# Sparse attention into a gated FFN: PSUM banks taken singly or in pairs, and a new order for the first 420 tasks

## The chip, the cores and the metric

The kernel runs on one core of a Trainium2 chip. A core has five engines that run side by side, each through its own queue of instructions in order: PE (TensorE, matrix products), ACT (ScalarE, functions of one input), DVE (VectorE, elementwise work and reductions), POOL (GpSimd, here only the issue of loads) and SP (SyncE, here the issue of stores and of transposes by DMA). They hand work on through semaphores. PE writes into PSUM, eight banks of 128 partitions by 512 float32 values; ACT and DVE read it from there. A *whole-array* matmul contracts over 128 rows; a *row tile* uses 64 rows, and two of them run side by side. The trace shows these as `128*128` and `64*128`.

The metric is the device time of one execution in microseconds (us), the median of several.

## The reference

Block-sparse attention over `q`, `k`, `v` of shape 4 x 8 x 768 x 64 (batch, heads, tokens, width), then a gated FFN on the 3072 x 512 tokens that come out of it:

```python
mask = np.abs(blk_i - blk_j) <= window          # blocks of 32 tokens
mask = mask | (blk_i == 0) | (blk_j == 0) | (blk_i == n_blocks - 1) | (blk_j == n_blocks - 1)
for qb in range(n_blocks):
    for kb in sampled_blocks[qb]:
        mask[qb * block:(qb + 1) * block, kb * block:(kb + 1) * block] = True
attn = softmax(where(mask, q @ k.T / 8, -1e9))
x = (attn @ v) as tokens x 512
gate = 1 / (1 + exp(-(x @ w_gate)))
out = (gate * (x @ w_val)) @ w_out              # 512 -> 1536 -> 512
```

## The kernel before

**Units.** The work is cut into twelve units: batch `b` of 4 times query third `u` of 3 (256 queries). In a unit the eight heads go by pairs `p` of 4. A pair has three steps `j` of 256 keys each. A step is: a score job on PE (`Step.qk`, L556 on), the exponential on ACT (L586, 128 x 1024 from two banks to float16), and a multiplication with the mask on DVE (L592). For the first unit the mask is a bias that PE adds ahead of the scores, so that a score job there has eight matmuls and no multiplication. When the three steps of a pair are done, PE forms the product with `v` (`Pair.pv` for the first two units, whole-array; `Pair.pv_parts` later, row tiles), DVE divides by the sums (`norm`, L655 and L656; before it `fold`, L646, for the later units), and the result is turned, by PE and a copy for the first two units (`turn`, `evac`), by a DMA transpose from SP later (`xbar`, L706). It lands in `xT`.

**FFN.** The units 0 to 3 have an FFN group each, the others go by two (`GROUPS`). `Ffn.f` takes 512 columns at a time: two tiles of 128 hidden values for a group of one unit, one tile for a group of two. Gate and value product go into the two banks of a pair, then `tanh` on ACT (L801) and the gating on DVE (L804) read both. `Ffn.y` multiplies by `wo`. Group 0 has whole-array jobs (`whole`), the others are row tiles in two rounds (`turns`: the second round changes the banks of the two row tiles and waits for the first). The first two jobs of group 0 start on three of four chunks of `xT` (`EARLY`).

**PSUM.** Four tiles `m0` to `m3` of two banks each (`units_ps`); a job takes one of the four (`Bank.slot`) until its last reader is done. Masks, transposes and spreads take a pair as well.

**Order.** `plan.add` only collects tasks: an engine with a time, a function, and what it depends on. `Plan.run` then issues them in the order of the string `ORDER`, written out by hand or by a program: a number is a task, `:2` the PSUM pair that it takes, a letter another engine than the first one named (`98A` copies mask columns on ACT), `@30` lets a load wait for task 30, and `j3` issues matmuls on zeros that only keep PE active. The times in `plan.add` and words such as `ops`, `lag` and `wide` are not used when it runs. Each engine's queue has its tasks in this order. An engine that waits holds all that is behind it. The loads' queue (POOL) starts with the first batch and the weights in the order of `FIRST`; loads, mask copies (L297 on ACT, L299 on DVE) and copies of `v` with a column of ones (`vcopy`, L545) are tasks like the others. The keys and queries of the later batches are copied by DVE (`pair_up`, L525) and transposed by DMA (`xbar`, L536).

## Time and profile before

| | |
|---|---|
| median of three runs | 279.34 us (279.06 to 279.7) |
| profiled execution | span 277.8 us; its page gives no time beside the span |
| busy in the span | PE 270.0 us, DVE 207.1, ACT 192.1, POOL 47.3 |
| instructions | PE 5007, DVE 421, ACT 243, POOL 69 |
| granted TensorE clock, mean | 0.999 |
| moved by DMA | 28.93 MB, 104 GB/s over the span |

The span runs from the first to the last instruction; the timed runs also have what lies around it. A row of a timeline gives the start, the time from there to the end, the engine, the line, the operation, the tiles (written <- read) and how many instructions were merged; the bracket is the idle time ahead of it and what ended that. A row of a group gives the busy time, the mean of one in ns, the idle time ahead of them and what ended it. PE's matmuls overlap in their pipeline, so the step from one start to the next is what one costs, not the row's length. Nearly all matmuls are issued through one helper (L352), so they are told apart by their tiles.

### The profile page before, as it was taken

The page shows a single profiled execution, that of the slowest core. Times are in us where ns is not written, and L with a number is a line of the kernel's source. Part 1 is how long each engine was busy: PE and PEld are TensorE (multiplying, and loading weights), DVE is VectorE, ACT ScalarE, POOL GpSimd, SP SyncE. Part 2 cuts the span into 40 slices and gives each one's busy share as a digit, 9 for nine tenths or more (in the row PEclk, how much of TensorE's full clock was granted, in tenths as well). Part 3 has the DMA queues.
Part 4 walks back from the last instruction along what each step waited for, and adds up shares of the span by engine and source line. Part 5 has one row for each costly group of instructions (what it writes and reads, how often), then busy time and mean ns, then how long its engine had stood idle before and what let it go on. Part 6 is the DMA issues. An engine that isn't in the chain of part 4 may idle for free.

```text
span 277.8 us, 11169 instructions
## 1 busy us (share of the span) xinstructions
PE 270.0 (97%) x5007; PEld 178.7 (64%) x5007; DVE 207.1 (75%) x421; ACT 192.1 (69%) x243; POOL 47.3 (17%) x69
## 2 busy tenths in 40 slices
PE   8879999999999999999999999999999999999995
PEld 3667785896897798655566655655655676555543
DVE  4667788899999989978988886887876899004422
ACT  3988868899989958968868965679688571035300
POOL 7776261030480000028300000000000000000000
PEclk9999999999999999999999999999999999999999
DMA  7999999994599693339986743014130002230004
GB/s 160 175 195 197 200 205 198 140 139 100 84 160 145 117 140 97 103 98 167 142 113 113 73 61 97 2 21 142 24 96 4 4 2 76 70 151 2 0 2 151
DMA packets 56684, 28.93 MB, mean 104 GB/s; under 512 B 33036, under 2 KB 53692, under 8 KB 56636
## 3 DMA queue, kind: packets, MB, share of 16 engines
q0 software_dynamic: 21520, 13.90, 35.7%
q1 hardware_dynamic: 34628, 14.02, 24.8%
q8 instruction: 39, 0.64, 1.0%
q10 hardware_dynamic: 488, 0.30, 0.3%
q14 instruction: 9, 0.07, 0.1%
HBM read 28.47 MB, written 6.29 MB: 125 GB/s over the span
## 4 chain that ended last, share of the span: by engine, by line
PE 87%; DMA 7%; POOL 2%; ACT 1%; DVE 1%; issue 1%; SPq 0%
PE m L352 86%; DMA q<-in_q_dram 3%; DMA v<-in_v_dram 2%; DMA kT<-kp 1%; ACT P L586 1%; POOL k L226 1%; POOL q L226 1%; POOL wg L236 0%; POOL wv L236 0%; DVE ysb L888 0%; DVE P L592 0%; ACT ysb L886 0%; PE m L472 0%; PE m L467 0%; ACT ysb L929 0%
## 5 line engine op out<-in xcount | busy, mean ns | idle before, releaser
L586 ACT ACTIVATE P<-m 128x1024 f16<-128x1024 f32 x144 | 143.1, 1025 | 27.8 <-PE m L352 24.6
L352 PE MATMUL m<-xT,wg 64*128 64x512 f16 (+2 forms) x720 | 136.7, 326 | 0.1
L352 PE MATMUL m<-xT,wv 64*128 64x512 f16 (+2 forms) x720 | 136.7, 326 | 0.0
L592 DVE TENSOR_TENSOR P<-P,mask 128x1024 f16<-128x1024 f16 x132 | 87.0, 684 | 2.7 <-ACT P L586 2.6
L352 PEld LDWEIGHTS <-wg 64*128 64x128 f16 (+1 forms) x720 | 66.6, 94 | 21.2 <-issue 0.8
L352 PEld LDWEIGHTS <-wv 64*128 64x128 f16 (+1 forms) x720 | 66.4, 94 | 18.2 <-issue 0.5
L804 DVE SCALAR_TENSOR_TENSOR ht<-th,m 128x512 f16<-128x512 f32 x72 | 49.0, 685 | 37.0 <-ACT th L801 36.1
L352 PE MATMUL m<-wo,ht 64*128 64x512 f16 (+2 forms) x564 | 70.4, 372 | 0.0
L801 ACT ACTIVATE th<-m 128x512 f32<-128x512 f32 x72 | 42.8, 598 | 29.6 <-PE m L352 26.1
L352 PE MATMUL m<-qT,kT 64*128 64x256 f16 x576 | 53.6, 269 | 0.9 <-DMA kT<-kp 0.5
L352 PEld LDWEIGHTS <-P 64*128 64x128 f16 (+1 forms) x2112 | 41.1, 94 | 5.2 <-issue 0.4
L352 PEld LDWEIGHTS <-ht 64*128 64x128 f16 (+1 forms) x564 | 29.4, 94 | 23.4 <-issue 1.3
L352 PE MATMUL m<-vex,P 64*128 64x65 f16 (+1 forms) x2112 | 42.5, 190 | 0.0
L352 PEld LDWEIGHTS <-kT 64*128 64x128 f16 x576 | 26.7, 94 | 17.8 <-issue 1.3
L646 DVE TENSOR_REDUCE acc<-m 128x260 f32<-128x520 f32 x40 | 27.8, 697 | 7.9 <-PE m L352 6.8
L226 POOL DMA_DIRECT2D k<-in_k_dram x15 | 11.1, 744 | 48.3 <-PE m L352 45.0
L886 ACT ACTIVATE ysb<-m 128x512 f32<-128x512 f32 x18 | 10.2, 601 | 11.8 <-PE m L352 11.8
L656 DVE TENSOR_TENSOR x<-acc,rz 128x256 f16<-128x256 f32 x40 | 17.0, 425 | 1.4
L226 POOL DMA_DIRECT2D v<-in_v_dram x16 | 11.6, 736 | 33.5 <-PE m L352 12.9
L226 POOL DMA_DIRECT2D q<-in_q_dram x19 | 13.9, 733 | 3.9 <-DMA wo<-in_moe_w_out_dram 1.8
L352 PE MATMUL m<-bias,e 64*128 64x256 f16 x48 | 5.9, 271 | 2.3 <-DVE mask L299 1.9
L929 ACT ACTIVATE ysb<-m 128x256 f32<-128x256 f32 x1 | 0.4, 383 | 10.1 <-PE m L352 10.1
(47 smaller groups left out, 84.1 us busy)
## 6 DMA issues: line engine op xcount, KB each, us to landing
out_dram<-ysb SPq DMA_DIRECT2D x23, 256.0 KB, 2.4
v<-in_v_dram POOLq DMA_DIRECT2D x16, 192.0 KB, 5.1
k<-in_k_dram POOLq DMA_DIRECT2D x15, 192.0 KB, 6.6
q<-in_q_dram POOLq DMA_DIRECT2D x12, 192.0 KB, 6.4
wg<-in_moe_w_gate_dram POOLq DMA_DIRECT2D x6, 256.0 KB, 8.4
wv<-in_moe_w_val_dram POOLq DMA_DIRECT2D x6, 256.0 KB, 9.0
wo<-in_moe_w_out_dram POOLq DMA_DIRECT2D x3, 512.0 KB, 12.8
xT<-x SPq DMA_TRANSPOSE x40, 2.4
```

The lines of the kernel that those rows point to most:

```text
L226: return nc.gpsimd.dma_start(dst[:, h0:h1, t0:t1, :], src[b, h0:h1].rearrange("h (p t) d -> p h t d", t=NT)[:, :, t0:t1, :],)
L352: return nc.tensor.matmul(out, lhsT, rhs, start=start, stop=stop, skip_group_check=True).ins
L586: nc.scalar.activation(self.pt.rearrange("a h i n -> a (h i n)"), both(self.bank).rearrange("a h n -> a (h n)"), AF.Exp, bias=0.0, scale=SCALE
L592: nc.vector.tensor_tensor(self.pt, self.pt, m.unsqueeze(1).broadcast_to([128, 2, 2, UQ]), op=ALU.mult,)
L646: nc.vector.tensor_reduce(self.acc.rearrange("a h s d -> a (h s d)"), self.parts.rearrange("a r n -> a n r"), axis=mybir.AxisListType.X, o ...
L656: nc.vector.tensor_tensor(self.x16.rearrange("a s h d -> a h s d"), self.acc[:, :, :, 0:D], rz.broadcast_to([128, 2, 2, D]), op=ALU.mult,)
L801: nc.scalar.activation(th, both(bank)[:, 0, :], AF.Tanh, bias=0.0, scale=0.5)
L804: nc.vector.scalar_tensor_tensor(self.ht[:, tiles[0] : tiles[-1] + 1, :], in0=th.rearrange("a (f n) -> a f n", n=self.w), scalar=1.0, in1= ...
L886: nc.scalar.activation(ysb, both(bank)[:, s, :], AF.Copy, bias=0.0, scale=0.5)
L929: nc.scalar.activation(ysb, src, AF.Copy, bias=0.0, scale=0.5)
```

## The change

PSUM becomes one tile of eight banks. A job takes a pair as before (`0` to `3`), or a single bank (`a` to `h`; `a` and `b` are the two banks of pair `0`). In a single bank:

- the FFN of the first two units goes by one tile of 128 hidden values, gate and value side by side in 2 x 256 columns, whole-array (`Ffn.f1`); for unit 1 this replaces row tiles in two rounds. `tanh` and gating have half the columns and are twice as many; their buffers are halves of the old ones (`th1`). `EARLY` is now 4 such tiles, as many hidden values as before;
- the product with `v` of the first two units is in one bank and not two (its matmuls are the same);
- transposes, masks and spreads can be whole-array in one bank, by the slot that the order gives them.

The order string is new. Its numbers differ because the list of tasks has 1205 entries where it had 1173. Told by what the tasks do, the first 420 stand in a new order, and behind them each engine has the old one but for places exchanged among a few neighbours. In the head nine mask copies are on DVE, where six were there and three on ACT; the copy of the mask's rows (`mb24`) and one first evacuation of a transpose moved from DVE to ACT, one cast the other way; and there are 12 pairs of matmuls on zeros where there were 19. The times in `plan.add` change throughout, and words such as `needs`, `one` and `mode` come in; none of them is used when the order runs.

```diff
-PE, ACT, DVE, DMA, SP = "PADGS"
+PE, ACT, DVE, DMA, SP, ONE = "PADGSQ"
-EARLY = 2
+EARLY, SMALL = 4, 2
 ORDER = """
-j3 j3 j3 j3 j3 j3 j3 j3 5A 8D j3 0 11A j3s 9:0 j3s j3s j3s 10D j3s j3s 12:1 1:2 j3s 13A 3:0 2 j3s 34:1 4D 35 15:2
+11A 5 j2 j2 j2 j2 j2 j2 j2 j2 j2s 6:0 j2 j2s 12:1 8 92 9:2 0 1:g 2 7A 10 3:0 j1s 15:3 13A 30:1 4A
+31 16 80Q:a 81 84Q:b 17:3 18 34:2 35 44:3 76:1 45 85 77 40:0 97:2 98 25Q:c 41 27Q:d 26 32:3 33 28
...
-    units_ps = [ps.tile([128, 2, 512], f32, name=f"m{i}") for i in range(4)]
+    banks = ps.tile([128, 8, 512], f32, name="m")
+    units_ps = [banks[:, 2 * i : 2 * i + 2, :] for i in range(4)]
...
+    def one(bank):
+        i = "abcdefgh".index(bank.slot)
+        return units_ps[i // 2][:, i % 2, :]
...
+    rings["th1"] = [t[:, c : c + UQ] for t in rings["th"] for c in (0, UQ)]
...
-    def halves(out16, tiles):
+    def turned_in(bank, tiles):
         for i, tile_ in enumerate(tiles):
+            flat = len(tile_.shape) == 2
+            if bank.single:
+                if flat:
+                    nc.tensor.transpose(one16(bank)[:, i * 128 : (i + 1) * 128], tile_, ident)
+                    continue
+                for h in range(2):
+                    nc.tensor.transpose(
+                        one16(bank)[h * D : (h + 1) * D, i * 128 : (i + 1) * 128],
+                        tile_[:, h],
+                        ident,
+                    )
+                continue
...
         def pv(self, eng):
-            acc = both(self.bank)[:, :, 0 : 2 * (D + 1)]
-            self.acc = acc.rearrange("a h (s d) -> a h s d", s=2)
+            self.acc = one(self.bank)[:, 0 : 4 * (D + 1)].rearrange(
+                "a (h s d) -> a h s d", h=2, s=2
+            )
...
+        def f1(self, f):
+            bank = Bank()
+            i = len(used["th1"])
+            th = home("th1", i)
+            def go(cs):
+                def mm(eng):
+                    for c in cs:
+                        for g in range(2):
+                            bank.last = tiled(
+                                one(bank)[:, g * UQ : (g + 1) * UQ],
+                                (wg, wv)[g][:, c, f * 128 : (f + 1) * 128],
+                                self.x[:, c, :],
+                                c == 0 and g == 0,
+                                c == 3 and g == 1,
+                            )
+                return mm
+            def tanh(eng):
+                nc.scalar.activation(th, one(bank)[:, 0:UQ], AF.Tanh, bias=0.0, scale=0.5)
+            def gate(eng):
+                nc.vector.scalar_tensor_tensor(
+                    self.ht[:, f, :],
+                    in0=th,
+                    scalar=1.0,
+                    in1=one(bank)[:, UQ : 2 * UQ],
+                    op0=ALU.add,
+                    op1=ALU.mult,
+                )
...
         def f(self, j):
+            if self.g < SMALL:
+                for f in range(self.per * j, self.per * (j + 1)):
+                    self.f1(f)
+                return
```

## The prediction

> **What bounds the kernel now.** I read the page's busy shares and its chain first, then the chain in order of time, then windows of 20 us, then the PE, ACT, DVE and POOL timelines of the first 45 us.

> ```profile
> PE 270.0 (97%) x5007; PEld 178.7 (64%) x5007; DVE 207.1 (75%) x421; ACT 192.1 (69%) x243; POOL 47.3 (17%) x69
> ...
> PE 87%; DMA 7%; POOL 2%; ACT 1%; DVE 1%; issue 1%; SPq 0%
> ...
> 15.57 8.08 DMA q<-in_q_dram
> ...
> 47.28 67.41 PE m L352 x1662
> ...
> 118.66 4.07 DMA kT<-kp
> ...
> 122.78 82.12 PE m L352 x1516
> ...
> 206.30 68.39 PE m L352 x884
> ```

> From 47 us to the end the chain is nearly all PE's own instructions, with one break of note: a transpose of K for which PE stands until 122.78. Before 24 us the chain runs through loads. So what the change does after the head is a matter of PE's work alone; what it does in the head is a matter of when PE fills up.

> ```profile
> 0.00:20.00 20.00, 16.51 (x339) 11.03 (x340) 12.09 (x32) 14.55 (x18) 14.87 (x25) 1.00 1.16 176
> 20.00:40.00 20.00, 19.42 (x322) 15.38 (x319) 15.17 (x35) 16.06 (x20) 10.87 (x15) 1.00 1.38 201
> 40.00:60.00 20.00, 20.00 (x452) 15.80 (x450) 17.16 (x38) 16.91 (x22) 2.86 (x4) 1.00 1.15 161
> 60.00:80.00 20.00, 20.00 (x496) 15.75 (x494) 18.84 (x39) 18.75 (x23) 6.69 (x10) 1.00 0.74 114
> 80.00:100.00 20.00, 20.00 (x462) 15.76 (x460) 18.80 (x40) 16.83 (x22) 2.64 (x4) 1.00 0.90 144
> ```

> The columns after the width are PE, PEld, DVE, ACT and POOL busy, granted clock, DMA share, GB/s. A busy PE may be a slow PE, so I count its work by start-to-start steps instead, and call the time that passed less the work done PE's lag.

> ```profile
> 13.20 0.26 PE L472 MATMUL m<-const,q 64*64 64x64 f16 x8
> 15.36 0.29 PE L352 MATMUL m<-bias,e 64*128 64x256 f16 x2 [1.91 <-DVE mask L299]
> 15.47 0.29 PE L352 MATMUL m<-qT,kT 64*128 64x256 f16 x2
> ...
> 18.54 0.90 PE L352 MATMUL m<-vex,P 128*128 128x65 f16 x24
> 19.38 0.39 PE L352 MATMUL m<-qT,kT 64*128 64x256 f16 x4
> ...
> 23.69 0.32 PE L472 MATMUL m<-const,q 64*64 64x64 f16 x16 [0.23 <-DMA q<-in_q_dram]
> 23.94 0.28 PE L352 MATMUL m<-xT,wg 128*128 128x256 f16 x1
> 24.06 0.27 PE L352 MATMUL m<-xT,wv 128*128 128x256 f16 x1
> ...
> 25.16 0.27 PE L352 MATMUL m<-xT,wv 128*128 128x256 f16 x1
> 25.36 0.23 PE L467 MATMUL m<-const,x 64*128 64x64 f16 x4
> ...
> 39.63 1.64 PE L352 MATMUL m<-vex,P 128*128 128x65 f16 x48
> 41.20 1.04 PE L352 MATMUL m<-wo,ht 64*128 64x512 f16 x8
> ```

> A 256-column step takes 0.11 (23.94 to 24.06; 15.36 to 15.47 for a pair of row tiles). So a score job of the first unit (eight matmuls, half of them the bias) is 0.43, a later one 0.22, an FFN tile of eight whole-array matmuls 0.88, a PV of a pair 0.73. A step from one tile size to another costs 0.10 more: 25.16 to 25.36 is 0.20 where 0.11 is the work; 18.54 to 19.38 is 0.84 where 0.73 is; 39.63 to 41.20 is 1.57 where two PVs are 1.46.

> Ahead of the first FFN matmul at 23.94 PE has done 12 x 0.433 + 4 PVs x 0.73 + 5 later scores x 0.217 + 6 masks x 0.11 + 1.4 of transposes, 0.4 of spreads, 0.2 of turns = 11.85. Its lag there is 12.1. From there to the first output matmul at 41.20 twelve changes of tile size and 0.3 of waits bring it to 13.6, and through the next stretch it stays at 13.65, since 40 to 100 us has PE busy throughout.

> Why the head lags, by the timelines of DVE, ACT and PE:

> ```profile
> 14.35 0.36 DVE L545 COPY vex<-v 128x768 f16<-128x768 f16 x1 [1.53 <-DMA v<-in_v_dram]
> 14.63 0.68 DVE L299 CAST mask<-m 128x512 f16<-128x512 f32 x1
> ...
> 21.09 0.17 DVE L655 RECIPROCAL rz<-m 128x4 f32<-128x4 f32 x1
> 21.30 0.42 DVE L656 TENSOR_TENSOR x<-m,rz 128x256 f16<-128x256 f32 x1
> 21.64 0.41 DVE L299 COPY qT<-m 128x512 f16<-128x512 f16 x1
> ```

> ```profile
> 8.56 0.59 ACT L297 CAST mask<-m 128x512 f16<-128x512 f32 x1
> 9.17 5.69 ACT L586 ACTIVATE P<-m 128x1024 f16<-128x1024 f32 x6
> 16.01 4.82 ACT L586 ACTIVATE P<-m 128x1024 f16<-128x1024 f32 x5 [1.15 <-PE m L352]
> ```

> ```profile
> 6.62 0.38 PE L472 MATMUL m<-const,k 64*64 64x64 f16 x24
> ```

> The first unit is ACT's: twelve exponentials, one each (5.69 - 1.02)/5 = 0.93. At 12.8 DVE meets a copy of v whose load lands at 14.3; the mask copy behind it (14.63) holds the bank that PE's next score wants, PE stands 1.91, ACT 1.15. Another 0.6 of ACT goes into a mask copy at 8.56.

> **The change, part by part.** *One PSUM tile.* The same eight banks under one name; each bank keeps its own order of writer and reader, so no wait is added by the name: 0. (If each access waited for the whole tile, PE's steps above would break everywhere; the built program's waits name instructions of the same bank.) The durations that `plan.add` carries do not enter the program: 0.

> *Order of the head.* In the new ACT queue the spread copy comes ahead of the first exponential, all nine mask copies are on DVE, and the v copies stand behind the loads they need. The new PE queue has k1's transposes ahead of the first score; k1 is there by 6.62 at the latest, so first exponential near 6.4 + 0.2 + 0.43 + 0.2 = 7.3, against 6.73 now. Twelve at 0.93 with some 0.3 of gaps end at 18.7, against 19.9 now (16.01 + 4 x 0.95). Behind the last stand on PE and DVE, in order: PV of pair 3 then pair 2 to 20.2; norm (21.09 to 21.64: 0.55, with 0.2 from PE's end) to 21.0; turn 0.2; its copy behind two others, 3 x 0.25, to 22.0; three scores run beside that. First FFN matmul at 22.15. The bounds: 21.3 if no exponential is late (start 6.73), and 23.94 if the DVE or load waits only move elsewhere.

> Work ahead of it: 12 x 0.433 + 4 x 0.73 + 6 x 0.217 + 5 whole-array masks x 0.216 + 4 x 0.11 + transposes 1.64 + spreads 0.43 + turns 0.40 = 13.40. Lag 22.15 - 13.40 = 8.75, against 12.1.

> *One-bank jobs.* A bank holds one FFN tile (gate and value side by side), so jobs run whole-array: 24 tiles x 0.88 = 21.1 against 21.0 now. k3, k2, q2, q3, three turns and five masks cost about double: +0.15, +0.15, +0.05, +0.05, +0.16, +0.53. With the FFN's 0.1, PE's work in all rises by 1.2. In the built order 22 changes of tile size follow the first FFN matmul up to the end of unit 1's FFN (16 of them before the first output matmul), against 12 now, since unit 1's FFN now is row-tiled like the scores. 22 x 0.10 = 2.2, all on PE, which is full there. So the lag settles at 8.75 + 2.2 + 0.2 = 11.15 against 13.65.

> [...] The trace agrees that a change costs, at 0.10, not all of the time that a matmul's row lasts beyond its step (0.28 - 0.11 = 0.17 at 23.94).

> *Smaller ACT and DVE pieces.*

> ```profile
> L804 DVE SCALAR_TENSOR_TENSOR ht<-th,m 128x512 f16<-128x512 f32 x72 | 49.0, 685 | 37.0 <-ACT th L801 36.1
> L801 ACT ACTIVATE th<-m 128x512 f32<-128x512 f32 x72 | 42.8, 598 | 29.6 <-PE m L352 26.1 <-DVE acc L646 2.7 <-DVE ht L804 0.8
> ...
> L931 DVE TENSOR_SCALAR ysb<-m 128x256 f32<-128x256 f32 x1 | 0.4, 425 | 1.0 <-PE m L352 1.0
> ...
> L929 ACT ACTIVATE ysb<-m 128x256 f32<-128x256 f32 x1 | 0.4, 383 | 10.1 <-PE m L352 10.1
> ```

> 24 gates near 0.425 for 12 of 0.685: DVE +2.0; 24 tanh near 0.383 for 12 of 0.598: ACT +2.0. DVE also takes three mask copies (+2.0) and gives the spread copy (0.96): +3.1 in all. ACT gives the former, 0.6 each, and takes the latter: about +1.0. Both lie beside PE: DVE's idle time in 20 to 100 us is 4.8 + 2.8 + 1.2 + 1.2 = 10.0, ACT's 11.4. Cost 0 while that cover holds; the other end is the second rival.

> *Loads.* POOL's queue is unchanged until the last weights, then batch 1's come in another order.

> ```profile
> 19.91 0.76 POOL L236 DMA_DIRECT2D wg<-in_moe_w_gate_dram  x1 [0.64 <-DMA wv<-in_moe_w_val_dram]
> ...
> 42.95 0.71 POOL L226 DMA_DIRECT2D q<-in_q_dram  x1 [1.81 <-DMA wo<-in_moe_w_out_dram]
> ```

> An issue waits for the load eight before it, so the first FFN weights are there at 19.9 and the last of wo at about 42.7. The job that needs that one stands behind 33.4 of work: lag at least 9.3, below 11.15. Hidden, with 1.8 to spare. SP's queue has the transposes of batch 1 by pairs 0, 3, 1, 2 where they were 0, 2, 1, 3; the scores that want them come by pairs 0, 1, 3, 2, the first behind 43.9 of work, at 55, some ten after its loads, the others from 62 on.

> *The rest.* Behind the first 420 tasks each engine's order is the old one but for places exchanged within a few tasks, so 0.75 at 122.78 and the last 3 us stay.

> **Sum.** 13.65 - 11.15 = 2.5 of lag won, 1.2 of work added: 1.3 faster. Against the profiled span 277.8 that is 276.5; the median of the timed runs lies 1.54 above that span, so 279.34 - 1.3 = 278.0.

> **Rivals.** (1) *More is won: changes of tile size fall into waits that PE has anyway.* Then the loads bound the lag, 9.3: 13.65 - 9.3 - 1.2 = 3.1 faster, 276.2; 0.10. Against it: in 24 to 41 us PE paid 0.10 for nearly each. (2) *DVE takes over as the bound between 40 and 100 us: slower.* It has 94% there. If DVE's +3.1 finds no idle time that it can use (waits for ACT can't be filled in order), PE is late by 3.1 at the banks that DVE frees: 279.3 + 3.1 - 1.3 = 281.1. It decides from 1.3 of the 3.1 on. For it: 1.2 idle per 20 us. Against it: the extra lies mostly before 60 us, where 7.6 is free; 0.16. (3) *The change does nothing: what is won is given back at the batch border.* PE stands 0.75 for kT at 122.78; if those transposes keep their time, it stands 2.05: 279.3. Against it: their loads and copies wait for work that moves along. With a first FFN matmul near 23.5 for a reason that I did not see, it comes to the same; 0.11. (4) *Changes of tile size cost the whole pipe where one-bank jobs follow row tiles*: 0.17 each, the 22 take 1.5 more, 279.5; 0.03, for the 0.10 is read from three kinds of change in this kernel. [...]

> **How the numbers follow.** 0.2% (0.56 us) is what a measurement of this kernel can tell from no change. The forecast has 0.60, with its own range from 277.0 (first FFN matmul at 21.3, less some waits) to 278.7. Faster: 0.60 + 0.10 = 0.70. Same: rivals 3 and 4, 0.14. Slower: 0.16. The range for 8 in 10 reaches from 276.6, leaving out the best part of rival 1, to 279.9, about half of rival 2.

> **What would show it.** First FFN matmul (128*128, xT) near 22.15, and no wait over 0.6 of PE between 8 and 22; the twelfth exponential's end near 18.7; the first wo matmul at about 41.1 behind 30.2 of work, a lag of 10.5 to 11.0; PE busy 20.0 in each window from 40 to 100. Wrong would be: PE idle there with DVE named, an exponential chain with gaps above 1 us, or steps over 0.15 at the changes of tile size.

## The result, and the profile after

The changed kernel is slower: 279.83 us (median of 20 runs, 278.62 to 281.40) against 278.60 us (20 runs, 277.79 to 281.06) for the kernel before, a ratio of 1.0035 with a 95% interval of 1.002 to 1.005. Forecast were 278.0 us and a gain of 1.3. That the time lies just inside the range, whose end is 279.9, is luck: the forecast started from 279.34, the median of three executions, and twenty have 278.60. Against the kernel before, the range ended at 0.6 slower, and measured are 1.0 (by the ratio) to 1.2 (by the medians). Single executions of either kernel spread over some 3 us, far more than the difference, so in what follows a trace says which waits there are, and medians say what they cost. Executions more than 1.5% above the fastest of the same kernel are left out of the ratios.

The profiled execution took 280.17 us, its span is 278.4. From the page, the busy shares and the shares of the chain:

```profile
PE 271.6 (98%) x4859; PEld 187.4 (67%) x4859; DVE 210.1 (75%) x437; ACT 190.6 (68%) x251; POOL 47.2 (17%) x69
...
PE 87%; DMA 7%; DVE 3%; issue 1%; SPq 1%; ACT 1%; DVEq 0%
```

DVE is 3.0 busier than before, where 3.1 was forecast, but that is luck too. By the groups' rows the gates cost 1.0 more (40.8 and 9.2 against 49.0) and not 2.0, and three output copies (`ysb`, at 48.8, 71.0 and 71.6), which ACT made before, are on DVE now, 1.9 more (4.6 against 2.7). Neither the account of the change nor the forecast has these. ACT, forecast some 1.0 busier, is 1.5 less busy. The shares look alike; the place of the waits does not. The windows of 20 us (columns as before: PE, PEld, DVE, ACT, POOL busy, granted clock, DMA share, GB/s):

```profile
0.00:20.00 20.00, 18.05 (x319) 12.18 (x320) 13.84 (x36) 15.02 (x18) 15.63 (x26) 1.00 1.15 170
20.00:40.00 20.00, 20.00 (x321) 15.55 (x318) 17.85 (x43) 19.40 (x28) 9.40 (x13) 1.00 1.38 200
40.00:60.00 20.00, 19.74 (x393) 15.03 (x391) 17.29 (x42) 13.48 (x23) 4.29 (x6) 1.00 1.25 160
60.00:80.00 20.00, 18.71 (x397) 14.83 (x396) 15.96 (x32) 16.30 (x23) 7.90 (x11) 1.00 1.11 150
80.00:100.00 20.00, 19.90 (x455) 16.23 (x449) 18.79 (x40) 17.38 (x21) 0.72 (x1) 1.00 0.59 98
```

PE is fuller in the first 40 us (38.05 against 35.93) and has holes from 40 to 100 us, where the kernel before had none; the DMA share of 60 to 80 us is 1.11 instead of 0.74. The chain in order of time (start, length, what) names the holes:

```profile
48.08 7.42 DMA qT<-qp
55.51 0.14 issue
55.64 2.67 PE m L366 x68
...
62.67 1.26 SPq L741
63.98 1.24 SPq L741
65.26 7.17 DMA xT<-x
...
72.47 6.57 PE m L366 x186
79.03 0.21 issue
79.24 5.27 PE m L366 x128
84.62 190.62 PE m L366 x3336
```

There are four: before a score at 55.64, whose q transpose was under way for 7.4; before the third group's FFN at 72.47, whose x transpose was under way for 7.2; and at 79.24 and 84.62, where the chain names nothing but "issue". From 84.62 to the end PE runs through.

In PE's lag (time passed less work done, as in the prediction), by the work done so far, in us:

```
work done            20     40     50     60     70     90    110    250
before            13.17  13.61  13.67  13.69  13.73  13.79  14.60  14.99
before, again     13.03  13.47  13.52  13.54  13.58  13.63  14.86  15.26
changed           10.41  11.34  12.05  13.40  13.83  14.17  14.21  14.37
changed, again    10.46  11.40  12.19  12.56  12.84  12.90  12.93  13.10
```

The changed kernel is 2 to 3 ahead at 20 and 40, and gives most of it back between 44 and 71 of work; the kernel before loses nothing there and 0.8 to 1.2 at the border of the batches. Carried from the profiled executions to the medians (each kernel's runs take 1.76 longer than their span: 0.33 less than the changed kernel's trace, 0.95 less than the first trace of before), both kernels end with the same lag, 14.0. What remains between them is PE's added work, 1.2.

### The profile page after: what moved, and what is told of

Same layout as the page of the kernel before. It is cut to its first block, busy times and chain, and to the rows that moved or that the text cites. A ratio compares the mean times of both kernels' runs of the same rounds, so it can differ in the third digit from the quotient of the medians.

```text
span 278.4 us, 10889 instructions
## 1 busy us (share of the span) xinstructions
PE 271.6 (98%) x4859; PEld 187.4 (67%) x4859; DVE 210.1 (75%) x437; ACT 190.6 (68%) x251; POOL 47.2 (17%) x69
## 4 chain that ended last, share of the span: by engine, by line
PE 87%; DMA 7%; DVE 3%; issue 1%; SPq 1%; ACT 1%; DVEq 0%
PE m L366 85%; DMA qT<-qp 3%; DMA xT<-x 3%; DMA k<-in_k_dram 2%; DVE P L628 1%; SPq L741 1%; ACT P L622 1%; DVE mask L304 1%; PE m L502 0%; PE m L489 0%; DVE acc L682 0%; DVE ht L834 0%; DVE kp L561 0%; PE m L486 0%; ACT ysb L1016 0%
## 5 line engine op out<-in xcount | busy, mean ns | idle before, releaser
L366 PEld LDWEIGHTS <-wg 64*128 64x128 f16 (+1 forms) x672 | 62.6, 94 | 19.7 <-issue 1.5
L366 PEld LDWEIGHTS <-wv 64*128 64x128 f16 (+1 forms) x672 | 62.5, 94 | 17.1 <-issue 1.7
L905 DVE SCALAR_TENSOR_TENSOR ht<-th,m 128x512 f16<-128x512 f32 x60 | 40.8, 685 | 33.9 <-ACT th L902 33.3
L902 ACT ACTIVATE th<-m 128x512 f32<-128x512 f32 x60 | 35.6, 597 | 27.1 <-PE m L366 23.0
L366 PEld LDWEIGHTS <-ht 64*128 64x128 f16 (+1 forms) x564 | 31.2, 94 | 22.0 <-issue 1.3
L366 PEld LDWEIGHTS <-kT 64*128 64x128 f16 x576 | 29.6, 94 | 15.7 <-issue 2.3
L682 DVE TENSOR_REDUCE acc<-m 128x260 f32<-128x520 f32 x40 | 27.9, 697 | 10.4 <-PE m L366 10.1
L974 ACT ACTIVATE ysb<-m 128x512 f32<-128x512 f32 x15 | 8.5, 599 | 11.7 <-PE m L366 11.7
L231 POOL DMA_DIRECT2D v<-in_v_dram x16 | 11.4, 716 | 21.4 <-PE m L366 21.2
L231 POOL DMA_DIRECT2D q<-in_q_dram x19 | 13.6, 716 | 6.0 <-PE m L366 5.2
L831 ACT ACTIVATE th<-m 128x256 f32<-128x256 f32 x24 | 8.2, 398 | 5.3 <-PE m L366 5.2
L834 DVE SCALAR_TENSOR_TENSOR ht<-th,m 128x256 f16<-128x256 f32 x24 | 9.2, 416 | 2.5 <-ACT th L831 2.3
## 6 DMA issues: line engine op xcount, KB each, us to landing
wv<-in_moe_w_val_dram POOLq DMA_DIRECT2D x6, 256.0 KB, 10.1
```

What stands on the lines that cost most here:

```text
L231: return nc.gpsimd.dma_start(dst[:, h0:h1, t0:t1, :], src[b, h0:h1].rearrange("h (p t) d -> p h t d", t=NT)[:, :, t0:t1, :],)
L366: return nc.tensor.matmul(out, lhsT, rhs, start=start, stop=stop, skip_group_check=True).ins
L682: nc.vector.tensor_reduce(self.acc.rearrange("a h s d -> a (h s d)"), self.parts.rearrange("a r n -> a n r"), axis=mybir.AxisListType.X, o ...
L831: nc.scalar.activation(th, one(bank)[:, 0:UQ], AF.Tanh, bias=0.0, scale=0.5)
L834: nc.vector.scalar_tensor_tensor(self.ht[:, f, :], in0=th, scalar=1.0, in1=one(bank)[:, UQ : 2 * UQ], op0=ALU.add, op1=ALU.mult,)
L902: nc.scalar.activation(th, both(bank)[:, 0, :], AF.Tanh, bias=0.0, scale=0.5)
```

## The experiments

Ratios are to the kernel before, on the same chip, as recorded with their 95% intervals; the quotient of the two medians differs from them by up to 0.003. Different experiments ran on different chips. In the diffs a number is a task of the order, a letter or digit behind a colon its bank, and a number behind @ the task that a load waits for.

### The theories

A: batch 2's loads hold the DMA engines, and the x transposes stand behind them. B: SP's queue holds the transposes. C: the border of the batches takes back whatever is won ahead of it. D, formed after the first four runs: whatever PE waits for by DMA between 44 and 90 us (transposes of q, k and x, and PE's own instructions) comes late beside loads in flight, and the new order needs these things sooner after their issue than the old one did.

### Loads of batch 2 later

```diff
-336@333 ... 464@363 ... 295@376 314@376 ... 366@373 353@373 ... 379@360 ... 350:3
+350:3 336@350 464@350 295@350 314@350 366@350 353@350 379@350
```

> The changed kernel, with seven loads of batch 2 (v and q, k, q, k of pairs 0, 1, 3, v of pair 1) let go by a score job that runs at 70.8 us, ahead of the third group's first FFN job's end, instead of by jobs between 63 and 70. Theory A (the transposes of unit 2's x, issued 62.7 to 66.5 on SP's queue, land as late as 72.4 because these loads go out at 64.0 to 71.5 and hold the DMA engines): the last of the four lands before 69, PE's 1.24 at 72.47 goes, PE's lag behind its work is 12.2 to 12.5 at the PV job that runs at 73.12 now (13.40 now), and the time falls by 1.0 to 1.6 against the changed kernel, to 278.2 to 278.8 where the changed one has 279.8. Theory B (SP's order holds them, since two transposes of batch 1 wait there for DVE until 61.3): they land 2.5 after their issue all the same, so at 67 to 69, and PE's step comes out alike; what speaks for B alone is a landing that stays at 72. Theory C (it isn't the third group's wait that costs; the 0.75 at the border of batch 1 and 2 takes back whatever is won): PE's wait at 72.5 goes, one as long comes at 115 to 125, the time stays within 0.2% of the changed kernel.

Measured: 280.10 us, 1.0045 [1.0021, 1.0069]. The wait at 72.5 is gone as A says, and nothing is gained. The chain of this kernel:

```profile
55.93 0.44 DVE x L692
56.37 27.23 PE m L366 x566
83.60 1.31 issue
84.91 7.11 PE m L366 x137
```

PE now stands 1.3 ahead of 56.37, where DVE's normalisation came last, and 1.31 for "issue" at 83.60, in the middle of the burst that had been moved there. The lag at 90 is 14.47 (14.17 without the edit), so neither A's gain of 1.0 to 1.6 nor C's wait at the border came.

### Unit 2's x first on SP

```diff
-258 ... 260 ... 250 ... 248 ... 327 ... 305
+258 ... 248 ... 327 ... 305 260 250
```

> The changed kernel with SP's queue alone reordered: the three transposes of unit 2's x (pairs 0, 3, 2) go ahead of the two transposes of batch 1's pair 2, which wait for DVE until 61.3 now. Theory A (the loads hold the DMA engines): x goes out at 59 to 62, before the loads of 64.0, and lands by 66, so PE's 1.24 at 72.47 goes; but the two transposes of pair 2 then go out at 63 to 65 and land with the loads at 70 to 73, and the scores that want them, at 69.7, wait 1 to 3: no gain, 279.3 to 280.8. Theory B (it is SP's order alone): x lands by 66, pair 2's transposes within 4 of their issue, by 69; PE waits nowhere before 78 and the time falls by 1.0 to 1.6, to 278.2 to 278.8.

Measured: 280.58 us (279.97 without one execution of 285.22), 1.0064 [1.0036, 1.0092]. It went as A said: x in time, pair 2's k late, by this row of PE's timeline (the wait stands in brackets):

```profile
71.36 0.39 PE L366 MATMUL m<-qT,kT 64*128 64x256 f16 x4 [1.12 <-DMA kT<-kp]
```

B falls: SP's order chooses which transpose is late, not whether one is.

### One PSUM tile alone

```diff
-units_ps = [ps.tile([128, 2, 512], f32, name=f"m{i}") for i in range(4)]
+banks = ps.tile([128, 8, 512], f32, name="m")
+units_ps = [banks[:, 2 * i : 2 * i + 2, :] for i in range(4)]
```

> The kernel before with one thing of the change: the four PSUM tiles of two banks become slices of one tile of eight banks; order, jobs and slots are the old ones. By the prediction (waits stay per bank): the same as before within 0.2%, with a lag of PE of 13.65 from 42 to 110. If the name cost anything (waits taken from whole-tile dependences), it is slower by 0.3% or more and PE stands in 40 to 100 us.

Measured: 279.28 us, 1.0012 [0.999, 1.0034]. PE's busy time is 20.00 in each window from 40 to 100 us, as in the kernel before; the name costs nothing that can be measured. Its one trace lost 2.3 at the border (111.4 to 124.4: 1.0 to DVE's `fold`, behind an x transpose in the chain, the rest to x and k transposes), which shows how far single executions of the old order, too, differ there.

### Both edits, and two loads of batch 1 later

```diff
 (both edits above)
-237@217 ... 181@217 ... 114@217 ... 296:d
+237@217 ... 296:d 181@296 114@296
```

The FFN's helper also returns its last matmul here, so that a load can wait for an FFN job.

> The changed kernel with both edits (loads of batch 2 let go at 70.8, unit 2's x ahead of pair 2's transposes on SP) and one more: two loads of batch 1 (k of pair 2, v of pair 0) let go by an FFN job at 52.6 instead of 45.5, so that the q transposes of 48.1 don't stand behind them until 55.5. Theory A: the waits of 0.39 at 55.64 and 1.24 at 72.47 go, PE's lag at 73 is 11.8 to 12.2, and if nothing takes it back the time is 277.9 to 278.4, 0.2% or so below the kernel before. Theory B: the same by the x transposes, but the 0.39 at 55.64 stays. Theory C (the border of the batches takes back what is won): a wait of 0.7 to 2 at 115 to 125 and a time above 279.

Measured: 280.90 us, 1.0070 [1.0043, 1.0098]. No wait for a transpose is left, and the lag at 70 is 12.26, but the time isn't the 277.9 to 278.4 that A gives. After 73:

```profile
71.90 11.05 PE m L366 x306
82.95 0.45 issue
83.40 6.14 PE m L366 x128
89.54 0.88 issue
90.42 1.59 PE m L366 x29
```

Two waits for "issue" bring it to 13.97. What they are, the DMA packets of the instruction queue tell. For the changed kernel the page has them in one row (packets, MB, share of 16 engines); with 9,738 recorded instructions of PE and its weight loads that is a packet of 16,384 bytes for each 256 of them:

```profile
q8 instruction: 38, 0.62, 0.9%
```

Between 24 and 130 us PE has 13 waits over 0.3 with no releaser in all traces of this study. For eight of them: after how many recorded PE instructions the wait stands, when PE passed the place 256 instructions before, and when the packet ran that was next (us). "PE stands" is from the start of the last instruction to the start of the next; the chain counts from the modelled end of the last and so shows up to 0.3 less:

```
kernel                after instr.    256 before      packet           PE stands
changed               2752            73.79           77.01 to 77.95   78.76 to 79.24
changed               3008            78.74           82.18 to 83.11   84.24 to 84.62
changed, again        2752            72.95           76.05 to 77.00   77.92 to 78.26
batch 2 later         3008            78.22           82.57 to 83.50   83.33 to 84.91
both edits            3008            77.57           81.08 to 82.03   82.68 to 83.40
both edits            3264            82.66           85.93 to 88.99   89.27 to 90.42
before, loads spread  4032            94.48           96.50 to 98.10   98.34 to 99.54
before, loads spread  4288            98.31          102.91 to 103.93 104.08 to 105.47
```

All 13 stand at 256 n + 192 recorded instructions, to the instruction: PE has come to the border of a page, and goes on 1.3 to 1.5 after the next packet has ended. These packets start 2.0 to 4.6 after the border before, and at that moment at least two loads that had gone out hadn't landed. A late packet alone doesn't stop PE: in the changed kernel the one of 53.41 starts 3.96 after its border (49.45), and PE, which takes until 56.61 for that page, runs on. So in these traces a packet runs while PE works on the page before, and mostly that is soon enough: in the changed kernel's first trace 18 of the 38 start between 24 and 130 us, and PE stops over 0.3 for two of them. Between 75 and 105 us it wasn't soon enough 13 times in these kernels, by 0.3 to 1.8 a time.

### Batch 2's loads spread out

```diff
 (SP's order and batch 1's loads as above)
+376:2 418@376 ... 360:2 295@360 ... 347:3 314@347 ... 458:0 366@458 ... 503:2 353@503 ... 475:1 397@475
+461:1 336@461 ... 489:1 379@489 ... 544:1 464@544 ... 556:0 443@556 ... 559:3 432@559
```

> The changed kernel with batch 2's twelve loads let go one by one, 2 to 4 us apart, by score jobs from 67 to 101 us (six of q and k first, v and pair 3 behind), unit 2's x ahead of pair 2's transposes on SP, and two loads of batch 1 at 52.6. Theory D (bursts of loads fill the DMA engines; what is small and late behind them, the transposes of q and x and PE's own instruction pages of 16 KB, stops PE, at one place or another according to where the burst stands): no wait of PE over 0.2 between 40 and 110, none at the page borders (256 PE instructions) either, PE's lag at 100 us 12.0 to 12.6 where the changed kernel has 14.1, and 1.3 to 2.0 faster than the changed kernel: ratio to before 0.997 to 0.999. Theory C (the border of batch 1 and 2 takes it back): the lag is 12.0 to 12.6 until 115, a wait of 1 to 2 stands at 115 to 125, and the ratio is 1.001 to 1.004. If bursts aren't the cause, pages come late as before and the lag at 100 stays near 14.

Measured: 282.57 us, 1.0107 [1.0067, 1.0146]; the same pacing in the kernel before (tasks 386, 271, 288, 334, 321, 365, 306, 347, 432, 411, 400 behind the matching scores):

> The kernel before with the same pacing of batch 2's loads as in the changed kernel with spread loads: one by one from 67 to 100. Theory D: little, 0 to 0.2% faster, since no wait of PE stands in 47 to 118 of the profiled run; if it gains as much as the changed kernel does (0.4% or more), the burst costs both kernels alike and the changed one's loss lies elsewhere.

281.50 us, 1.0084 [1.0052, 1.0116]. Both get worse, and the prediction of D fails in the form it had: it isn't the burst alone. In the changed kernel the loads now reach into the time of the next transposes, of which three go out at 98.78:

```profile
98.78 8.69 DMA kT<-kp
107.47 0.05 issue
107.52 0.50 PE m L366 x5
```

With a load each 2 to 5 us one that went out at 98.78 landed at 107.47. So in this trace it took no burst to make a transpose late. In the kernel before, the two stops at page borders in the table, 2.6 together, are most of what its trace loses. What D keeps is the rest: loads and what PE waits for had better not run at the same time. The old order comes closer to that: in its first trace unit 2's x goes out from 63 to 69, and batch 2's loads follow:

```profile
71.62 0.71 POOL L226 DMA_DIRECT2D v<-in_v_dram  x1 [10.53 <-PE m L352]
72.33 2.16 POOL L226 DMA_DIRECT2D k<-in_k_dram  x3
```

### Both kernels without batch 2's loads

```diff
-lambda eng: load_heads(dst, src, b, 2 * p, 2 * p + 2),
+lambda eng: None if b == 2 else load_heads(dst, src, b, 2 * p, 2 * p + 2),
```

> The changed kernel without batch 2's twelve loads (the q, k and v of batch 1 are used again for batch 2: the output is not the reference's). Theory D: with no burst between 64 and 90 the waits at 72.5, 78.8 and 84.2 go (1.24 + 0.39 + 0.28); the 0.42 at 55.6, which stands behind loads of batch 1, stays; 1.5 to 2.0 faster than the changed kernel. Theory C: they go, and 1 to 2 comes back at 115 to 125, unless that border's wait hung on the loads too.

> The kernel before without batch 2's twelve loads (batch 1's data are used again). Theory D as it stands says that the kernel before lost nothing to its burst from 71 to 90 in the profiled run: the same as before within 0.2%, or up to 0.3% faster if other runs lose what the profiled one did not. The difference between the changed kernel and this one, both without loads, is what the head is worth by itself: the prediction's terms give 1.3 faster for the changed one, the lags read in its trace (1.5 won, 1.2 of work added) give 0.3.

Both leave out the loads of batch 2 and use batch 1's data in their place.

Measured: the changed kernel 278.76 us, 0.9997 [0.9969, 1.0024]; the kernel before 278.43, 0.9976 [0.9951, 1.0001]. Without these loads the changed kernel has no wait over 0.4 left after the head, in the profiled execution. What it loses against the kernel before is 0.2% by the ratios where it was 0.35%, and 0.3 us by the medians where it was 1.2. With intervals of some 0.3% each way that is no proof that the loss shrinks, and in three of these 12 executions the clock fell as told below. C isn't borne out here: no wait comes at 115 to 125. Nor is the changed kernel ahead, as the lags of the head would have it. The head of the profiled execution shows something else, in windows:

```profile
6.00:7.00 1.00, 0.00 (x0) 0.00 (x0) 0.33 (x1) 1.00 (x2) 1.00 (x2) 1.00 1.41 195
7.00:8.00 1.00, 0.97 (x30) 0.78 (x32) 0.39 (x1) 0.04 (x1) 1.00 (x3) 0.53 1.41 184
8.00:9.00 1.00, 1.00 (x10) 0.64 (x6) 0.17 (x1) 0.43 (x1) 1.00 (x2) 0.50 1.40 160
```

PE stood 1.11 for the k of pair 1, and then the granted clock (third column from the right) was 0.5 until 13.9, worth 2.9 of lag at 20, the gap included (13.31 for 10.41). More of that below.

### The changed kernel once more

> The changed kernel once more, unaltered, for a second trace. Theory D (DMAs that PE waits for come late behind loads in flight: q and x transposes and PE's own pages of 256 instructions): PE's lag rises from 11.2 to 11.8 at 40 us of work to 13.6 to 14.7 at 90, by two to four waits of which each ends with a transpose of q, k or x or stands at a page border (10.75 or 11.75 times 256 recorded PE instructions), not necessarily the same ones as in the first trace; ratio 1.002 to 1.005. If the waits of the first trace were an accident of that execution, the lag at 90 is below 13.

Measured: 279.76 us, 1.0037 [1.0013, 1.0061]. PE stands at the same places (until 55.77, 71.63, and 78.26 at instruction 2752), for shorter: 0.49, 0.26, 0.25. The lag at 90 is 12.90, below the 13.6 to 14.7 of D and just in the range that was set for an accident. So the places come again, and the lengths of the first trace don't. At the first place something else came last this time, a gate on DVE, 0.1 after the q transpose:

```profile
55.77 0.39 PE L366 MATMUL m<-qT,kT 64*128 64x256 f16 x4 [0.33 <-DVE ht L834]
```

### Paced between the transposes, without and with junk

```diff
 (SP's order and batch 1's loads as above)
+360:2 418@360 ... 405:0 295@405 314@405 ... 347:3 366@347 ... 406 353@406 ... 440:2 397@440
+419:3 336@419 ... 458:0 379@458 ... 451:1 464@451 ... 486:3 443@486 ... 503:2 432@503
```

> The changed kernel with the three edits of the run that had all of them (two loads of batch 1 at 52.6, unit 2's x ahead of pair 2's transposes on SP, batch 2's loads behind pair 2's scores), but with the twelve loads of batch 2 let go one by one, 1.2 us apart, from 69 to 80 us: after unit 2's transposes and before unit 3's, so that neither meets a load, and with fewer loads in flight at a time than when they went out in one burst. Theory D: no wait for transposes in 50 to 90, pages late by less than 2, so PE's lag at 90 us of work 12.2 to 13.0 (13.98 with the burst), and a ratio of 0.995 to 0.999. If pages come late whenever loads are in flight at all, however few, the lag at 90 is 13.5 to 14.5 and the ratio 1.002 to 1.006.

Measured: 279.70 us, 1.0038 [1.0013, 1.0063]. One wait is left (1.20, k of pair 2 at 70.3), no page is late enough to stop PE, the lag at 90 is 12.90 as D says, and still the ratio isn't the 0.995 to 0.999 of D: no gain in the median. With three more pairs of junk matmuls ahead of the k of pair 1 (`j1 j1 j1s j1` for `j1s`):

> The same with three more pairs of junk matmuls (512 wide, some 0.64 in all) in the gap in which PE waits for batch 0's k of pair 1 before the first score. In the changed kernel without batch 2's loads PE stood 1.1 there and the granted clock then was 0.5 from 7.0 to 13.5 us, which cost the head 2.3. If it is that gap that lets the clock fall, no execution of this kernel has a granted clock below 0.997, where a quarter of those of its relatives on two chips had 0.988 to 0.994, and its median is 0.2 to 0.6 below that of the paced kernel without them; a head without the fall is at most 0.3 later than now.

Measured: 280.70 us, 1.0060 [1.0033, 1.0087]: worse by 1.0. The junk doesn't end before 7.6 where k is there at 6.7, the first FFN matmul moves from 22.64 to 23.94. No clock fell in either, so the pair tells nothing on that.

### Unit 1's FFN over pairs of banks again

```diff
-EARLY, SMALL = 4, 2
+EARLY, SMALL = 4, 1
```

with the six row-tiled jobs in the places of the twelve.

> The changed kernel with one part of the change undone: unit 1's FFN in six row-tiled jobs over pairs of banks, as before the change, in the places of its twelve one-bank jobs. The prediction's price: some eight changes of tile size fewer at 0.10, 0.8 of PE's time between 50 and 64 us, and about 1.0 less of DVE and ACT each; if that is all, 0.5 to 0.9 faster than the changed kernel (ratio 1.000 to 1.002). Theory D: what is won there is lost again at the waits between 55 and 90, so it is within 0.2% of the changed kernel (1.002 to 1.005).

Measured: 281.23 us, 1.0086 [1.0056, 1.0116]. Each second half, adjacent to its first, began 0.23 late (it changes the banks of the two row tiles), 1.4 in all, so it was run once more with another job between the halves:

> The changed kernel with unit 1's FFN in row-tiled jobs over pairs of banks again, now with another job of PE between the first and the second half of each (in the run before this one they were adjacent, and each second half began 0.23 late, 1.4 in all). The prediction's price of the one-bank jobs (0.8 of tile-size changes, 1.0 of DVE and ACT): a ratio of 1.000 to 1.002. Theory D: 1.002 to 1.005. If one-bank jobs are a gain here (banks come free singly), 1.005 or more.

Measured: 283.31 us, 1.0151 [1.012, 1.0183]. PE's waits from 24 to 130 us (us in total, times, longest):

```profile
PE m L365 <- DMA qT<-qp: 1.4, 1, 1.4
PE m L365 <- ACT P L621: 1.0, 2, 0.7
PE m L365 <- DVE ht L904: 0.8, 2, 0.5
PE m L365 <- ACT th L901: 0.7, 1, 0.7
```

The first is again a transpose. The others, 2.5 in all, are waits for banks that ACT and DVE have not yet freed: a job that needs two banks waits for the later one. In this order the one-bank jobs are a gain, of up to 1.2% (a pair job in an order that is written for single banks is at its worst). Nothing here says that these jobs make the changed kernel slower; an order written for pair jobs wasn't run.

### Everything from 46 to 85 us kept apart

```diff
-284 285 ... 258 ... 260 ... 249 250 ... 248
+284 249 285 260 250 ... 258 ... 248
-114@217
+296:d 114@296
+363:3 418@363 ... 376:2 295@376 ... 373:0 314@373 ... 412:3 366@412 ... 360:2 353@360 ... 405:0 397@405
+347:3 336@347 ... 440:2 379@440 ... 419:3 464@419 ... 458:0 443@458 ... 486:3 432@486
```

> The changed kernel with everything in 46 to 85 us kept apart: the copy and both transposes of batch 1's pair 2 go ahead of unit 2's x on DVE and SP (57 instead of 60 to 62), v of batch 1's pair 0 is loaded at 52.6, and batch 2's loads go out one by one from 64.7 to 80. Theory D: no wait over 0.3 of PE between 50 and 90 us, PE's lag at 90 us of work 12.0 to 12.6, the ratio 0.996 to 0.999. If one wait of about 1 still comes at one of these transposes or page borders, the lag is 13 to 14 and the ratio 1.002 to 1.005: then it isn't their place in the order but how close to need the changed order has them all.

Measured: 278.79 us, 0.9996 [0.9975, 1.0016]: 0.4% better than the changed kernel by the ratios, level with the kernel before. Forecast were 0.996 to 0.999. From 24 to 130 us PE has a single wait, at a page border (instruction 3008, packet 81.42 to 82.35):

```profile
PE m L366 <- issue: 0.6, 1, 0.6
```

The last three loads then were moved past that page (464@475, 443@426, 432@472), once with the first eight 2 us later, too:

> The kernel with everything kept apart, its last three loads of batch 2 at 83, 86 and 88 us, and the first eight 2 us later (67.8 to 76), clear of unit 2's x. Theory D: the page whose border is at 11.75 times 256 instructions starts before 80.5 (81.42 with all loads out by 79.4), PE doesn't stand at 83, its lag at 90 us of work is 12.3 to 12.7 and the ratio 0.994 to 0.998: faster than both kernels. Against it: the three late loads meet unit 3's x transposes (83 to 91), and a wait of 0.5 to 1.5 comes between 88 and 108: ratio 0.999 to 1.004.

> The kernel with everything kept apart and only the last three loads of batch 2 moved, to 83, 86 and 88 us. Theory D: as in the other run for the page at 83 us, ratio 0.995 to 0.998; if the page comes as late as before (81 or later) though no load went out after 76, its lateness isn't the loads'.

Measured: 279.88 us, 1.0017 [0.9984, 1.005], and 280.07 us (279.77 without two executions of 282.78 and 401.58), 1.0031 [0.9999, 1.0062]. Neither is the 0.994 to 0.998 of D. The page comes at 81.00 and 80.11, PE doesn't stop at 83, and the lag grows from 40 to 90 by 0.6 and 0.8 only (by 2.8 and 1.5 in the changed kernel). The page's lateness goes with the loads: its packet starts 3.7 after the border where they go out up to 79.4, 2.1 where the last before it goes out at 78.0, and 1.1 where it does at 76.3, by one trace each. But in both traces PE stood for k in the head, and the clock fell:

```profile
PE m L502 <- DMA k<-in_k_dram: 1.0, 1, 1.0
```

```profile
8.00:10.00 2.00, 2.00 (x24) 1.18 (x20) 1.20 (x4) 1.02 (x1) 2.00 (x4) 0.50 1.32 161
```

(the first kernel's waits, and one of its windows). By the mean clock it fell in 3 of 12 executions of the first kernel and in 5 of 12 of the second; one of these, the one of 401.58 us, has a mean of 0.658, for which no trace gives a reason. The executions that kept the clock have a median of 278.31 in the first kernel, 0.5 below the kernel before, and of 279.45 in the second, 0.6 above it.

### The first of these, with a little junk in the gap

```diff
-3:0 j1s 15:3
+3:0 j1s j1 j1s j1s 15:3
```

> The kernel with everything kept apart and the last three loads late, with one wide and two narrow pairs of junk matmuls more (0.37 in all) in PE's gap before the k of pair 1, which is 0.5 in most executions and 0.9 to 1.1 in those whose clock fell. If the fall comes from that gap: no execution with a granted clock below 0.997, a median of 278.0 to 278.7 where the kernel before has 278.8, ratio 0.997 to 0.9995. If executions with 0.992 to 0.994 go on, the gap isn't the cause. If none falls and the median still lies at 279.5 or above, the waits from 50 to 110 come back in other executions than the profiled one.

Measured: 278.70 us against 279.30, 0.9987 [0.9958, 1.0016]. No clock fell in 12 executions, but they ran on another chip than the kernel without this junk, so that the junk did it isn't shown. Eight of them lie at 278.05 to 279.2, four at 280.1 to 280.5; the profiled one is of the latter, and lost 1.6 where theory C and the prediction's third rival have it:

```profile
119.75 4.11 DMA kT<-kp
123.85 0.05 issue
123.90 6.10 PE m L366 x103
```

This is the best version of the changed kernel, 0.5% below it by the ratios; that it beats the kernel before isn't shown.

### The kernel before once more

> The kernel before, unaltered, for a second trace: a ratio of 1 within 0.2%. If the copy of v that waits for its load (1.91 in the first trace) was an unlucky execution, PE's wait at 13.4 to 15.4 is 0.5 to 1.2 here and its lag at 40 us of work 12.6 to 13.1 instead of 13.6. The wait for kT near 122 stays, 0.5 to 1.0, and the lag at the end is 13.3 to 14.6.

Measured: 278.50 us, 0.9984 [0.9958, 1.001]. The longest wait of its head, the one for the mask copy behind the copy of v:

```profile
PE m L352 <- DVE mask L299: 1.4, 1, 1.4
```

1.4 is between the 1.9 of the first trace and the 0.6 of the one without batch 2's loads (whose head is the same). So the first trace was no unlucky exception, against the forecast of 0.5 to 1.2 and a lag at 40 of 12.6 to 13.1. Five traces of this head have a lag at 40 of 13.61, 13.79, 12.70, 12.78 and 13.47, a mean of 13.3, and the first FFN matmul at 23.0 to 24.1. The largest of these lags goes with a wait of 0.6 here and one of 0.9 for q, so the wait for v isn't the only term that varies.

## Why the prediction was wrong, step by step

- *One tile: 0.* Right (1.0012, and the interval holds 1).
- *PE's work: 1.2 more.* Right, and as large as the whole difference.
- *A change of tile size: 0.10.* Right. The first FFN matmul and the first of the output matmuls are these rows:

```profile
22.95 0.28 PE L366 MATMUL m<-xT,wg 128*128 128x256 f16 x1
...
41.46 0.81 PE L366 MATMUL m<-wo,ht 64*128 64x512 f16 x6
```

  The lag goes from 9.55 to 11.25 with 16 changes between them: 0.106 each. Forecast were 22.15 and 41.1. Rivals 1 and 4 fall with this.
- *The head: 2.5 of lag won.* Mis-sized; 1.8 by the means at 40 us of work (13.3 for five traces of the old head, 11.46 for eight of the new one at full clock). Two terms. The old head's 13.65 was one execution's, with the longest of the waits for v. And the new head was timed by ACT's chain alone:

```profile
7.69 12.77 ACT L622 ACTIVATE P<-m 128x1024 f16<-128x1024 f32 x13 [0.41 <-PE m L366]
```

  It starts 0.4 later than forecast, for k was there at 6.7 and not before, and its twelfth exponential ends at 19.39, not 18.7. But it isn't what sets the first FFN matmul: PE is, without a gap from 10.5 on. Between 10.48 (lag 7.18) and 22.95 (9.55) it makes 16 changes of tile size, 1.7 of these 2.4. I priced the changes behind the first FFN matmul and left those ahead of it at nothing, under a cover that the change had itself removed.
- *Smaller pieces for ACT and DVE: 0 while their cover holds; rival 2.* DVE is not the bound from 40 to 100 us. But at one place it is as late as the transposes: of PE's wait at 55.6 to 56.4 it came last in three traces (the changed kernel again, batch 2's loads later, x first), and the q transpose, which landed within 0.2 of that each time, in the first trace of the changed kernel. Which of the two costs there isn't told apart. Going back to pair jobs costs more.
- *Loads: hidden, with 1.8 to spare; the scores' transposes "some ten after its loads".* This step failed. It compared the landing of loads with the need for them and let the transposes on SP's queue and PE's instructions pass for free. In the new order the last loads of batch 1's k go out at 46 to 48 and batch 2's from 64 on. Three views of the changed kernel: SP's timeline, the rows of the x and q transposes among the DMA issues (last number: median us from issue to landing), and POOL's timeline (in brackets what it waited for):

```profile
48.08 5.44 SPq L572 DMA_TRANSPOSE qT<-qp  x3
...
62.67 3.83 SPq L741 DMA_TRANSPOSE xT<-x  x3
```

```profile
xT<-x SPq DMA_TRANSPOSE x40, 2.6
...
qT<-qp SPq DMA_TRANSPOSE x12, 4.1
```

```profile
64.05 1.43 POOL L231 DMA_DIRECT2D v<-in_v_dram  x2 [4.30 <-PE m L366]
65.47 0.72 POOL L231 DMA_DIRECT2D q<-in_q_dram  x1
68.02 0.72 POOL L231 DMA_DIRECT2D k<-in_k_dram  x1 [1.82 <-PE m L366]
```

  The first q transpose of 48 and the last x of 65 take 7.4 and 7.2 where the medians are 4.1 and 2.6, and the third group's FFN wants that x at 71; the old order let these loads go from 71.6 on, behind its x. 1.5 to 2.8 of lag goes between 40 and 90 of work in the two traces. By the medians the sum is: 1.8 won by the head (13.3 less 11.5), 1.2 of work lost, and 1.8 lost to waits behind the head, 2.5 from 11.5 to the lag of 14.0 at the end against 0.7 in the kernel before. That is 1.2 slower. The prediction had put these waits of the changed kernel at nothing but the border's 0.75.
- *The rest: 0.75 at the border stays; rival 3.* In the changed kernel's two traces the border's wait is gone; PE comes there some 0.3 to 1.6 later, which may be why. Where the waits before it were removed it came back in one trace (1.6), not in the others. So rival 3 was near: what the head wins is given back, but at the transposes and pages from 55 to 85 us and not at the border, and the added work comes on top, so that the change is slower and not level.

Four kernels keep loads, transposes and pages apart. Two of them win back 1.1 to 1.3 (0.9996 and 0.9987 against 1.0035, with intervals that don't overlap that of the changed kernel's first 20 executions); the other two, in which the clock fell in some executions, don't show it (1.0017 and 1.0031). Why a transpose or a page is so slow beside a load stays open: the DMA share is 1.2 to 1.3 while the two transposes above are under way, and 0.85 from 76 to 83, when two pages come late.

## What to carry to other kernels

A step that brings PE forward brings it nearer to every transfer that it will wait for later: list each one (loads, transposes, the pages of its own instructions), with its issue, its landing and PE's need, not only the loads that the change moves. Price each kind of cost over the whole stretch that the change makes dense, also where a wait covers it before the change. And before a difference of 0.5% is built on one trace, ask how far the terms in it (here the wait for v, 0.6 to 1.9) differ from execution to execution.
